# Row-halved projection matmuls in the last two attention units, joined value products and VectorE copies in the last one

## The chip, the cores and the metric

The kernel runs on one core of one Trainium2 chip. The metric is device time in microseconds (us) of one execution; three executions were timed and the median is given. The profile is of one further execution of the same program. Engines are named as in the profile: PE is TensorE's matmuls, PEld its weight loads, DVE is VectorE, ACT is ScalarE, POOL is GpSimd, SP is SyncE.

## The reference, cut to what matters

A transformer block in float32: pre-norm attention with 32 heads of 20 columns over 2048 tokens of width 640, then a pre-norm SwiGLU feed-forward of width 1728.

```
h  = x + attention(layernorm(x)) @ wo          # softmax over 2048 keys, 32 heads
h2 = h + (silu(n @ w_gate) * (n @ w_up)) @ w_down   # n = layernorm(h)
```

The change touches the stretch in which the last heads' attention runs while the first tokens' output projection (`@ wo`, added to x), their layernorm, and the transposition of the normed tokens for the feed-forward are already under way.

## The kernel before

**Stages.** The first stage (up to about 330 us) makes queries, keys and values. The second is attention. The third, from about 1471 us, finishes the projection and runs the feed-forward.

**Units and key tiles.** Attention runs over 32 units `u` (0 to 31): a unit is a group of four heads and a chunk `c` of 512 query tokens, `u = 4 * group + c`. Each unit has 16 key tiles `kt` of 128 keys. For every key tile PE makes four score products (`scores`, L1336: contraction over 62 rows, in one or the other half of the 128 rows, 512 columns, each into a `ps_one` bank of four), ACT takes the exponential of each (`probs`, L1342), and PE weighs the values with the probabilities of the key tile before (`weigh`, L1346: four products of 128 rows and 32 output columns each, which the trace shows as eight instructions). Finished probabilities wait in the list `todo`; `weigh_next` takes the oldest entry. The pool of `probs` has six tiles, two for each key tile.

**Row maxima.** Softmax needs the row maxima of a unit ahead of it. They come from further products (`max_one`, L229, 60 rows in one half, 512 columns) into a bank of `ps_max`, which DVE reduces (L235). `ps_max` has three banks in rotation. Three such products go into each key tile until all are done, which is in unit 30 after about ten key tiles; unit 31 has none.

**Order in a key tile.** PE's order is written out by hand: a string of `ORDER` for each key tile, of which s and S are score products in the lower and upper half of the rows, m and M maxima in the lower and upper half, and W is the weighing; with no maxima left it is `sSsSW`. After the weighing, at W, one entry of the list `extra` is issued.

**`extra`.** In units 30 and 31 it holds the output projection, norm and transposition of the chunks 0 and 1 (`projection(0, ...)` in unit 30, `projection(1, ...)` in unit 31): eight steps `first` in key tiles 0 to 7 (each a `project` of 128 tokens and one half of the 640 output columns), three steps of norm moments in key tiles 8 to 10, one empty step, and four `flip` steps in key tiles 12 to 15. A `project` issues 15 matmuls of 128 rows by 320 columns (L1070) into one `ps_max` bank; then DVE adds the sum to `h` (L1076), takes its moments (L1077), and after the second half of the columns combines them (L1079). A `flip` first issues the norm of the next token tile on DVE (`apply`, L1090), then five transposes (L1102) into two `ps_max` banks, and `split` copies each bank with ACT into a rounded high part and lets DVE subtract for the low part (both at the helper's lines L88 and L89).

In order on PE, in every key tile of units 30 and 31 that has a `project`: score and maximum products, W, 15 projection products. The next tile's score products follow. What stands behind the attention on PE is the projection of chunk 2 (`projection(2, ps_b)`), whose first product starts at 1470.88 us. The banks for it belong to a new pool, opened after the last weighing.

Of the kernel before, what the change touches and what calls it, by code (L numbers as in the profile page):

```python
# [9 lines left out]
F32 = mybir.dt.float32  # L10
# [4 lines left out]
ALU = mybir.AluOpType  # L15
AX = mybir.AxisListType

P = 128
# [5 lines left out]
ND = D // P  # L24
NT = S // P
CH = 512
NC = S // CH
# [7 lines left out]
ROW = P // 2  # L35
HALF = D // 2
# [11 lines left out]
def tile_block(ctx: ExitStack, tc: tile.TileContext, x, wqkv, wo, wg, wu, wd, out):  # L48
    nc = tc.nc
    x = x[0]  # L50
    out = out[0]
# [35 lines left out]
    def split(src, hi, lo, lo_engine=nc.vector):  # L87
        nc.scalar.activation(hi, src, AF.Copy)  # L88
        lo_engine.tensor_tensor(out=lo, in0=src, in1=hi.bitcast(F32), op=ALU.subtract)  # L89
# [38 lines left out]
    NU = NG * NC  # L128
# [906 lines left out]
        nc.gpsimd.tensor_copy(hi, raw)  # L1035
        nc.gpsimd.tensor_tensor(out=lo, in0=raw, in1=hi.bitcast(F32), op=ALU.subtract)

    def projection(c, ps_of):

        loaded, zs = {}, {}  # L1040
        mv = mvs[c] = moments_of[c // 2][:, c % 2]
        st = pe1.tile([P, TPC, 2, 6], F32, name=f"st{c}")
        rs = []

        def load(t):
            rows = slice((c * TPC + t) * P, (c * TPC + t + 1) * P)
            o = pc.tile([P, ND, P], F32, name="o_t", tag="o_t")
            nc.sync.dma_start(o, o_d[:, rows].rearrange("(k p) n -> p k n", p=P))
            loaded[t] = o

        def load_x(first=0, last=TPC):
            for t in range(first, last):
                rows = slice((c * TPC + t) * P, (c * TPC + t + 1) * P)
                nc.sync.dma_start(h_c[c][:, t, :], x[rows, :])

        def part(t):
            o = loaded[t]
            o_hi = pc.tile([P, ND, P], F32R, name="o_hi")
            o_lo = pc.tile([P, ND, P], F32R, name="o_lo")
            split(o, o_hi, o_lo, nc.gpsimd)  # L1060
            loaded[t] = (o_hi, o_lo)

        def project(t, half):
            o_hi, o_lo = loaded[t]
            hs = slice(half * HALF, (half + 1) * HALF)
            ps = ps_of()
            n = 0
            for a, w in ((o_hi, wo_hi), (o_hi, wo_lo), (o_lo, wo_hi)):
                for k in range(ND):
                    nc.tensor.matmul(  # L1070
                        ps[:, :HALF], a[:, k, :], w[:, k, hs],
                        start=(n == 0), stop=(n == 3 * ND - 1),
                    )
                    n += 1
            h = h_c[c][:, t, hs]
            nc.vector.tensor_tensor(out=h, in0=ps[:, :HALF], in1=h, op=ALU.add)  # L1076
            nc.vector.bn_stats(st[:, t, half, :], h)  # L1077
            if half == 1:
                nc.vector.bn_aggr(mv[:, t, :], st[:, t])  # L1079

        def moments(i):
            if i == 0:
                r, steps = rstd_steps(pc, mv[:, :, 1], TPC, "c")
                rs[:] = r, steps
            for f in rs[1][6 * i : 6 * i + 6]:
                f()

        def apply(t):
            z = zs[t] = pc.tile([P, D], F32, name="z2")
            nc.vector.tensor_scalar(  # L1090
                z, h_c[c][:, t, :], mv[:, t, 0:1], rs[0][:, t : t + 1],
                op0=ALU.subtract, op1=ALU.mult,
            )

        def flip(t):
            if t + 1 < TPC:
                apply(t + 1)
            z = zs.pop(t)
            for k0, k1 in ((0, 4), (4, 5)):
                ps = ps_of()  # L1100
                for k in range(k0, k1):
                    nc.tensor.transpose(  # L1102
                        ps[:, (k - k0) * P : (k - k0 + 1) * P], z[:, k * P : (k + 1) * P], ident
                    )
                if k1 < ND:
                    src = ps.rearrange("p (q k n) -> p q k n", q=2, n=P)
                    dst = both_of(z2_c[c])[:, :, t]
                    split(src, dst[:, :, 0], dst[:, :, 1], nc.vector)
                else:
                    dst = rest_of(z2_c[c])[:, t]  # L1110
                    split(ps[:, :P], dst[:, 0], dst[:, 1], nc.vector)

        def first(t, half):
            project(t, half)
            if half == 0 and t + 1 < TPC:
                part(t + 1)
            if half == 0 and t + 2 < TPC:
                load(t + 2)

        return (  # L1120
            [lambda: load(0), lambda: load(1), lambda: part(0)],
            [lambda t=t, half=half: first(t, half) for t in range(TPC) for half in range(2)],
            [lambda: moments(0), lambda: moments(1), lambda: apply(0)],
            [lambda t=t: flip(t) for t in range(TPC)],
            load_x,
        )
# [290 lines left out]
    for u in range(NU):  # L1417
        g, c = divmod(u, NC)
        if g == NG - 1 and c >= 2:
            _, first, ln, flips, _ = ahead  # L1420
            extra = [*first, *ln, lambda: None, *flips]
        for kt in range(NT):
            now[0] = u * NT + kt
            ready = [v for v, at in closing.items() if at == now[0]]
            probs = [pp.tile([P, 2, CH], F32, name="probs") for _ in range(2)]
            heads = [[0, 2], [1, 3]]
            order = ORDER[now[0] % len(ORDER)] if singles[0] or singles[1] else "sSsSW"
            for op in order:
                if op in "mM":
                    next_max(int(op == "M"))  # L1430
                elif op in "sS":
                    scores(u, kt, heads[op == "S"].pop(0), probs)
                else:
                    if todo:
                        weigh_next()
                    while ended:
                        max_all(ended.pop())
                    for v in ready:
                        max_finish(v)
                    if extra:  # L1440
                        extra.pop(0)()
                    if preparing and u and kt not in (3, 4) and quiet[0] != now[0]:
                        preparing.pop(0)()
                    if now[0] == (NU - NC) * NT + 8:
                        unit_ring, last_ring = weight_rings()
                        unit_ring.fill()
                        last_ring.fill()
            todo.append((u, kt, probs))
            if kt == 2 and u + 3 < NU:
                load_queries(u + 3)  # L1450
            if kt == 10 and u == 0:
                fill_ones(k_stk[1])
            if kt >= 8 and kt % 2 == 0 and c == 1 and g + 1 < NG:
                load_keys(g + 1, slice((kt - 8) // 2 * CH, (kt - 6) // 2 * CH))
            if kt >= 8 and kt % 2 == 0 and c == 2 and g + 1 < NG:
                load_values(g + 1, (kt - 8) // 2 * TPC, (kt - 6) // 2 * TPC)

            sooner = u >= NU - 2
            if kt == (3 if sooner else 4) and tail:
                reciprocals(u - 1, tail[0][2], nc.sync)  # L1460
                rb = spread(u - 1, nc.sync)
            if kt == (6 if sooner else 9) and tail:
                store_o(u - 1, tail[0][1], rb, nc.gpsimd, None)
            if kt == (7 if sooner else 11) and tail:
                store_o(u - 1, tail.pop()[1], rb, None, nc.sync)
            if g == NG - 1 and c >= 1:
                at = 8 if sooner else NT - 4
                if kt == at:
                    ahead = projection(
                        c - 1, ps_max if c < NC - 1 else (lambda: ps_b())  # L1470
                    )
                if kt in (at, at + 1, 12 if sooner else 14):
                    ahead[0][min(kt - at, 2)]()
                    if kt == at + 1 and c < NC - 1:
                        ahead[4]()
            k = 2 * (u - NU + 8)
            if kt in (12, 13) and 0 <= k + kt - 12 < ND:
                if k + kt == 12:
                    assert not preparing
                    wo_hi = pc.tile([P, ND, D], F32R, name="wo_hi", bufs=1)  # L1480
                    wo_lo = pc.tile([P, ND, D], F32R, name="wo_lo", bufs=1)
                load_wo(k + kt - 12)
            if kt in (2, 3) and 0 <= k + kt - 4 < ND:
                split_wo(k + kt - 4)
# [4 lines left out]
    u, o, r = tail.pop()  # L1489
# [6 lines left out]
    def ps_b():  # L1496
        return psum2.tile([P, CH], F32, name="ps_b", tag="ps_b", bufs=4)
# [551 lines left out]
```

## Time and profile before

| | us |
|---|---|
| median of three executions | 2038.6 (2038.28 to 2039.58) |
| the profiled execution, its own time | 2035.66 |
| span of the profiled execution, first to last instruction | 2033.9 |
| mean granted TensorE clock | 0.997 |
| PE busy | 2008.8 (99%) |
| DVE busy | 1612.6 (79%) |
| ACT busy | 1462.4 (72%) |
| POOL busy | 785.7 (39%) |

Busy PE counts pipelined matmuls from modelled start to end, so that PE looks busy in a drain too; how long a stretch takes is read from the starts of instructions. In the timeline a row is a run of like instructions of one engine: start, time to the end of the last, engine, line, operation, output and inputs, shapes, count, and in brackets the idle time before it with what ended it. A table by stretches gives for each engine the busy time and the count of instructions.

### The profile page before, as it was taken

The numbers are of one execution on the slowest core, as the hardware profiler recorded it, in microseconds if no ns is written. First come the engines' busy times: TensorE is split into PE (matmuls) and PEld (weight loads), VectorE is DVE, ScalarE is ACT, GpSimd is POOL, SyncE is SP. The second block draws the span as 40 slices with busy tenths as digits, with TensorE's granted clock in tenths as the row PEclk, the third lists the DMA queues.
The fourth block names the chain that finished last, engine by engine and source line by source line (L and its number), as shares of the span: only waits on it lengthen the run. The fifth ranks groups of instructions, "written<-read, shape, count | busy, mean of one in ns | idle before, by whom it ended". The sixth has DMA issues, their size and how long they took to land. (4 is left out here: it accounts for less than half of the span.)

```text
span 2033.9 us, 39129 instructions
## 1 busy us (share of the span) xinstructions
PE 2008.8 (99%) x13716; PEld 1238.9 (61%) x13716; DVE 1612.6 (79%) x3241; ACT 1462.4 (72%) x2952; POOL 785.7 (39%) x1079
## 2 busy tenths in 40 slices
PE   7999999999999999999999999999999999999999
PEld 6899996333333333333333333345598888888888
DVE  6678788888888888888888888885377666676677
ACT  3788988999999999999999999987633222211221
POOL 5554450334434334344430011011145454744555
PEclk9999999999999999999999999999999999999999
DMA  7776663343443534444433123211158654974642
GB/s 227 243 222 186 203 185 100 113 128 99 150 124 113 163 123 138 129 141 146 141 126 109 30 65 80 83 62 49 41 193 292 222 193 156 346 272 159 202 151 95
DMA packets 205124, 305.03 MB, mean 150 GB/s; under 512 B 47664, under 2 KB 82480, under 8 KB 203904
## 3 DMA queue, kind: packets, MB, share of 16 engines
q1 hardware_dynamic: 204832, 302.53, 45.9%
q8 instruction: 109, 1.79, 0.4%
q14 instruction: 87, 0.71, 0.1%
q10 hardware_dynamic: 96, 0.00, 0.0%
HBM read 205.78 MB, written 95.68 MB: 148 GB/s over the span
## 5 line engine op out<-in xcount | busy, mean ns | idle before, releaser
L1342 ACT ACTIVATE probs<-ps_one 128x512 f32<-128x512 f32 x2048 | 1056.9, 615 | 62.0 <-PE ps_one L1336 24.2
L235 DVE TENSOR_REDUCE mx<-ps_max 128x1 f32<-128x512 f32 x1472 | 925.4, 684 | 116.2 <-PE ps_max L229 64.1
L1336 PE MATMUL ps_one<-q_stk,k_stk 62*128 62x512 f32 x2048 | 583.5, 431 | 1.2 <-DVE mx L199 1.2
L1346 PE MATMUL acc<-probs,v_stk 128*32 128x512 f32 x4096 | 546.7, 605 | 0.0
L229 PE MATMUL ps_max<-k_stk,q_stk 60*128 60x512 f32 x1472 | 488.7, 440 | 0.1
L1336 PEld LDWEIGHTS ps_one<-q_stk,k_stk 62*128 62x128 f32 x2048 | 290.5, 185 | 284.7 <-ACT probs L1342 269.7
L229 PEld LDWEIGHTS ps_max<-k_stk,q_stk 60*128 60x128 f32 x1472 | 245.2, 185 | 165.4 <-DVE mx L235 126.9
L1729 DVE TENSOR_TENSOR tmp<-ps_a,tmp 128x512 f32<-128x512 f32 x208 | 141.3, 690 | 122.1 <-PE ps_a L1514 96.4
L1346 PEld LDWEIGHTS acc<-probs,v_stk 128*32 128x32 f32 x4096 | 80.6, 108 | 181.7 <-issue 169.5
L1608 PE MATMUL ps_b<-halves,yp 128*128 128x320 f32 x1032 | 179.0, 308 | 1.5 <-POOL yp L89 1.3
L1608 PEld LDWEIGHTS ps_b<-halves,yp 128*128 128x128 f32 x1032 | 165.2, 188 | 17.5 <-POOL yp L89 1.5
L1514 PE MATMUL ps_a<-t,units 128*128 128x512 f32 x624 | 162.5, 396 | 0.0
L246 POOL CAST both<-neg 128x16 fp32r<-128x16 f32 x32 | 6.6, 207 | 361.6 <-PE ps_one L1336 153.7
L1514 PE MATMUL ps_a<-z,units 128*128 128x512 f32 x516 | 133.9, 394 | 0.0
L89 POOL TENSOR_TENSOR yp<-y,yp 128x256 fp32r<-128x256 f32 x96 | 60.2, 627 | 189.8 <-ACT yp L88 189.8
L1514 PEld LDWEIGHTS ps_a<-t,units 128*128 128x128 f32 x624 | 112.6, 188 | 18.5
L1613 DVE TENSOR_TENSOR h<-ps_b,h 128x320 f32<-128x320 f32 x248 | 110.0, 482 | 6.9 <-PE ps_b L1608 5.4
L216 DVE CUSTOM_DVE_ANT_0 q_stk<-ps_single,q_stk 128x512 f32<-128x512 f32 x143 | 95.7, 689 | 22.4 <-ACT q_stk L222 15.0
L1514 PEld LDWEIGHTS ps_a<-z,units 128*128 128x128 f32 x516 | 93.1, 187 | 16.0
L556 PE MATMUL ps_one<-z_hi,w_hi 64*128 64x512 f32 x380 | 99.1, 402 | 1.8 <-ACT z_hi L88 1.7
L88 ACT ACTIVATE yp<-tmp 128x512 fp32r<-128x512 f32 x40 | 25.3, 632 | 103.2 <-POOL tmp L1601 103.2
L1381 POOL TENSOR_TENSOR o<-o,rb 128x512 f32<-128x512 f32 x31 | 39.9, 1286 | 152.9 <-ACT probs L1342 55.8
(221 smaller groups left out, 3017.9 us busy)
## 6 DMA issues: line engine op xcount, KB each, us to landing
units<-w_d SPq DMA_DIRECT2D x186, 256.0 KB
w_d<-stage SPq DMA_DIRECT2D x106, 256.0 KB
halves<-j_d SPq DMA_DIRECT2D x70, 320.0 KB
k_stk<-qk_d SPq DMA_DIRECT2D x112, 160.0 KB
j_d<-stage SPq DMA_DIRECT2D x42, 320.0 KB
q_stk<-qk_d SPq DMA_DIRECT2D x64, 160.0 KB
k_stk<-qk_d SPq DMA_DIRECT2D x112, 80.0 KB
rb<-r_d SPq DMA_DIRECT2D x32, 256.0 KB
```

The lines of the kernel that those rows point to most:

```text
L89: lo_engine.tensor_tensor(out=lo, in0=src, in1=hi.bitcast(F32), op=ALU.subtract)
L216: nc.vector.tensor_tensor_reduce(out=place, in0=pss[1], in1=place, scale=1.0, scalar=LEAST, op0=ALU.add, op1=ALU.max, accum_out=mx[:, b, p ...
L229: nc.tensor.matmul(ps, queries[u][rows, pair, t * P : (t + 1) * P], keys[u // NC][rows, pair, kc * CH : (kc + 1) * CH], start=True, stop=True,
L235: nc.vector.tensor_reduce(mxs[u][:, b, pair, t, kc : kc + 1], ps, axis=AX.X, op=ALU.max)
L556: product = nc.tensor.matmul(job["ps"][:, :out], lhs, rhs, start=(half == 0 and i == 0), stop=(half == 1 and i == job["n"] - 1),)
L1336: nc.tensor.matmul(ps, keys[u // NC][rows, p, kt * P : (kt + 1) * P], queries[u][rows, p, :], start=True, stop=True,)
L1342: nc.scalar.activation(probs[p][:, b, :], ps, AF.Exp, scale=scale)
L1346: nc.tensor.matmul(acc[32 * j : 32 * j + 32, :], values[u // NC][:, kt, j * VW : j * VW + 32], probs[j // 2][:, j % 2, :], start=(kt == 0) ...
L1514: nc.tensor.matmul(ps.rearrange("p (t n) -> p t n", t=TPC), w[k][:, i], z[k][:, :, j], start=(first and m == 0), stop=(last and m == len(n ...
L1608: nc.tensor.matmul(ps, a, b, start=(n == 0), stop=(n == len(pairs) - 1))
L1613: nc.vector.tensor_tensor(out=h, in0=ps, in1=h, op=ALU.add)
L1729: add = lambda out, ps, x: nc.vector.tensor_tensor(out=out, in0=ps, in1=x, op=ALU.add)
```

## The change

Three edits.

1. `projection` gets an argument `halved`. With it `project` makes each of its 15 products as two, one over the rows 0 to 63 and one over the rows 64 to 127, each row half into a bank of its own, the two halves in turn; DVE then adds both banks to `h`, one after the other. It is set for chunks 0 and 1, so in units 30 and 31; chunks 2 and 3 keep whole products.
2. In unit 31 the weighing is done in even key tiles only, two entries of `todo` there (one in key tile 0, which finds one entry), none in odd key tiles but the last, which takes one.
3. In `flip` of chunk 1 (unit 31) the copy of the high part is DVE's instead of ACT's; chunk 0 keeps ACT.

```
-    def projection(c, ps_of):
+    def projection(c, ps_of, halved=False):
...
             hs = slice(half * HALF, (half + 1) * HALF)
-            ps = ps_of()
+            rows = [slice(b * ROW, (b + 1) * ROW) for b in range(2)] if halved else [slice(0, P)]
+            pss = [ps_of() for _ in rows]
             n = 0
             for a, w in ((o_hi, wo_hi), (o_hi, wo_lo), (o_lo, wo_hi)):
                 for k in range(ND):
-                    nc.tensor.matmul(
-                        ps[:, :HALF], a[:, k, :], w[:, k, hs],
-                        start=(n == 0), stop=(n == 3 * ND - 1),
-                    )
+                    for r, ps in zip(rows, pss):
+                        nc.tensor.matmul(
+                            ps[:, :HALF], a[r, k, :], w[r, k, hs],
+                            start=(n == 0), stop=(n == 3 * ND - 1),
+                        )
                     n += 1
             h = h_c[c][:, t, hs]
-            nc.vector.tensor_tensor(out=h, in0=ps[:, :HALF], in1=h, op=ALU.add)
+            for ps in pss:
+                nc.vector.tensor_tensor(out=h, in0=ps[:, :HALF], in1=h, op=ALU.add)
             nc.vector.bn_stats(st[:, t, half, :], h)
...
                     dst = both_of(z2_c[c])[:, :, t]
-                    split(src, dst[:, :, 0], dst[:, :, 1], nc.vector)
+                    hi, lo = dst[:, :, 0], dst[:, :, 1]
                 else:
                     dst = rest_of(z2_c[c])[:, t]
-                    split(ps[:, :P], dst[:, 0], dst[:, 1], nc.vector)
+                    src, hi, lo = ps[:, :P], dst[:, 0], dst[:, 1]
+                if c == 0:
+                    split(src, hi, lo, nc.vector)
+                else:
+                    nc.vector.tensor_copy(hi, src)
+                    nc.vector.tensor_tensor(out=lo, in0=src, in1=hi.bitcast(F32), op=ALU.subtract)
...
                 else:
-                    if todo:
-                        weigh_next()
+                    both = u == NU - 1 and kt < NT - 1
+                    for _ in range(2 * (1 - kt % 2) if both else 1):
+                        if todo:
+                            weigh_next()
...
                     ahead = projection(
-                        c - 1, ps_max if c < NC - 1 else (lambda: ps_b())
+                        c - 1, *((ps_max, True) if c < NC - 1 else (lambda: ps_b(),))
                     )
```

## The prediction, made before the changed kernel ran

> **What bounds the kernel now.** I read the table by stretches first, cut at the key tiles that matter: the eight tiles of unit 30 with a projection, the rest of unit 30, the eight tiles of unit 31 with a projection, and the rest up to the first product behind the attention. The columns are time, then PE, PEld, DVE, ACT and POOL busy with counts, clock and DMA.
>
> ```profile
> 1361.70:1398.96 37.26, 37.26 (x244) 23.80 (x240) 22.31 (x45) 19.20 (x37) 5.98 (x4) 1.00 0.26 83
> 1398.96:1418.61 19.65, 19.54 (x126) 7.83 (x123) 12.61 (x31) 18.91 (x42) 2.53 (x3) 1.00 0.01 4
> 1418.61:1449.64 31.03, 31.03 (x210) 20.86 (x206) 7.75 (x18) 17.97 (x35) 5.96 (x4) 1.00 0.20 57
> 1449.64:1470.88 21.24, 20.50 (x126) 7.40 (x125) 10.05 (x26) 19.96 (x42) 1.55 (x1) 1.00 0.01 1
> ```
>
> PE is full and ACT half idle wherever a projection runs (stretches 1 and 3); ACT is the bound in the other two (18.91 of 19.65, 19.96 of 21.24). So one change meets two regimes. Behind 1470.88, the same view over the rest of the program:
>
> ```profile
> sum 564.00, PE 555.45 PEld 487.95 DVE 395.89 ACT 131.97 POOL 297.61; mean PE 50.50 PEld 44.36 DVE 35.99 ACT 12.00 POOL 27.05
> ```
>
> PE has 8.6 us of 564 free and nothing else is full: a shift of the attention's end goes through to the end one for one. The sum below is therefore the shift of that end.
>
> Next the timeline of unit 30, PE alone and DVE alone, for the steps of one tile; the waits of PE's weight loads; and mean durations from the page.
>
> ```profile
> 1363.27 0.90 PE L1070 MATMUL ps_max<-wo_hi,o_lo 128*128 128x320 f32 x5
> ...
> 1365.42 1.06 PE L1346 MATMUL acc<-probs,v_stk 128*32 128x512 f32 x8
> 1366.42 0.85 PE L1070 MATMUL ps_max<-wo_hi,o_hi 128*128 128x320 f32 x4
> ```
> ```profile
> 1364.20 0.49 DVE L1076 TENSOR_TENSOR h<-ps_max,h 128x320 f32<-128x320 f32 x1 [2.45 <-PE ps_max L1070]
> 1364.73 0.49 DVE L1077 BATCH_NORM_STATS2 st<-h 128x6 f32<-128x320 f32 x1
> 1365.14 1.87 DVE L235 TENSOR_REDUCE mx<-ps_max 128x1 f32<-128x512 f32 x3
> ...
> 1369.97 0.21 DVE L1079 BATCH_NORM_AGGREGATE mvs<-st 128x2 f32<-128x12 f32 x1
> 1370.10 1.83 DVE L235 TENSOR_REDUCE mx<-ps_max 128x1 f32<-128x512 f32 x3
> ```
> ```profile
> PEld ps_max L229 <- DVE h L1076: 2.1, 6, 0.4
> ```
> ```profile
> L235 DVE TENSOR_REDUCE mx<-ps_max 128x1 f32<-128x512 f32 x1472 | 925.4, 684 | 116.2 <-PE ps_max L229 64.1 <-PE ps_one L1336 48.3
> L1336 PE MATMUL ps_one<-q_stk,k_stk 62*128 62x512 f32 x2048 | 583.5, 431 | 1.2 <-DVE mx L199 1.2
> L1346 PE MATMUL acc<-probs,v_stk 128*32 128x512 f32 x4096 | 546.7, 605 | 0.0
> ```
>
> Already now a maximum product waits for the bank that DVE's add has to empty (six times, up to 0.4 us): with three `ps_max` banks, DVE's queue is nearly on PE's path.
>
> **Edit 1, the halves themselves.** Whether two row halves stream side by side is shown by the first stage:
>
> ```profile
> 302.32 0.31 PE L556 MATMUL ps_one<-w_lo,z_hi 64*128 64x320 f32 x1
> 302.41 0.66 PE L556 MATMUL ps_one<-w_hi,z_lo 64*128 64x320 f32 x6
> ```
>
> One such half product lasts 0.31, six of both halves 0.66, so they start (0.66 - 0.31) / 5 = 0.07 apart, 0.14 for a pair. A whole product steps by (0.90 - 0.31) / 4 = 0.147 (row at 1363.27). Thirty halves cost what fifteen whole ones do, 2.2 us. What can be gained is at the end:
>
> ```profile
> 1424.29 0.90 PE L1070 MATMUL ps_max<-wo_hi,o_lo 128*128 128x320 f32 x5
> 1425.12 0.76 PE L1336 MATMUL ps_one<-q_stk,k_stk 62*128 62x512 f32 x4
> 1425.81 1.06 PE L1346 MATMUL acc<-probs,v_stk 128*32 128x512 f32 x8
> 1426.80 0.42 PE L1070 MATMUL ps_max<-wo_hi,o_hi 128*128 128x320 f32 x1
> ```
>
> The last whole product starts at 1424.29 + 0.59 = 1424.88, the scores 0.24 later instead of one step of 0.147; and the second pair of scores starts 0.76 - 0.43 = 0.33 after the first, against about 0.23 where halves run on (estimate: 0.147 x 512/320), 0.10 more. Halves are of the scores' kind, so both go: 0.09 + 0.10, taken as 0.195 for a projection, 1.6 us for eight.
>
> **Edit 1 in unit 30, the banks.** Let P be the start of the last projection product, 1363.27 + 0.59 = 1363.86. DVE's add starts P + 0.34, the moments 0.53 later, the first reduction 0.41 after that, the others by (1.87 - 0.68) / 2 = 0.60. The next projection starts at 1366.42 = P + 2.56. Its bank is that of the first maximum, whose reduction ends at 1365.14 + 0.68 = P + 1.96. No wait.
>
> Now the projection takes two of three banks, the three maxima take the third and then those two, and the next projection wants the banks of the first and the second maximum. DVE's queue has a second add, which needs the first one's result; I price that as moments after add, 0.53. So: first add P + 0.34, second 0.87, moments 1.40, reductions 1.81 and 2.41, the second ending at 3.09. With 0.05 for PE to see it (an estimate: DVE sees PE's end, 1363.86 + 0.31, within 0.03) the second half starts at P + 3.14, not 2.56. PE works in order, so the first half's next product, the rest of this projection and the next scores are queued behind it. From there 2.16 us to the new P as now (1361.70, where the first stretch is cut, to 1363.86). The cycle is 5.30; after a second column half the combining (0.53 after the moments if priced like them, the reductions 0.13 after it, instead of 0.41) adds 0.25: 5.55. Eight projection tiles take 37.26 now, 4.66 each. Over seven cycles: 4 x 5.30 + 3 x 5.55 - 7 x 4.66 = **+5.2 us**. The 0.195 is inside this, since PE comes earlier and waits longer; the eighth tile's is used up by the third maximum, which waits for the second add. Bounds: -1.6 if no bank is late, +6.5 if the third maximum delays the weighing by another 0.2 in each cycle. I take 5.2: every term is a row, and the cycle closes on itself.
>
> A sentence of the Trainium skill speaks to this. In "TensorEngine Tiling (Array Packing)", section "Gotcha 1: PSUM Pressure", it says that row tiles write to different banks and cannot use one bank at the same time. Without that rule one bank and one add would do and unit 30 would gain 1.6; with it, it loses 5.2; no run here shows two halves in one bank at once.
>
> **Edit 1 in unit 31.** No maxima, DVE idle (7.75 of 31.03): the gain stands, **-1.6 us**.
>
> **Edit 2, tiles 0 to 8.** A weighing takes 1.00 to the next kind of product, two passes of (1.06 - 0.61) = 0.45 in it. A second one directly behind costs 0.91 and saves a change into weighing (last scores to weighing 0.36 instead of 0.23, from 1425.12 + 0.33 to 1425.81: 0.13) and the slow first steps after it (0.1 each for projection and scores): 0.4 a pair. But in an odd tile two projections are only 0.47 of scores apart: the second one's second bank is free at 0.34 + 0.49 + 0.05 = 0.88 after the last product, PE is there at 0.147 + 0.47 = 0.62. That gives back 0.26. Four pairs: **-0.6 us** (between 0 and -1.6).
>
> **Edits 2 and 3, tiles 8 to 15.** Here ACT is the bound:
>
> ```profile
> 1453.73 1.04 PE L1336 MATMUL ps_one<-q_stk,k_stk 62*128 62x512 f32 x4
> ...
> 1457.80 1.04 PE L1336 MATMUL ps_one<-q_stk,k_stk 62*128 62x512 f32 x4
> 1458.78 1.06 PE L1346 MATMUL acc<-probs,v_stk 128*32 128x512 f32 x8
> 1459.77 0.76 PE L1102 MATMUL ps_max<-ident,z 128*128 128x128 f32 x5
> 1460.47 0.73 PE L1336 MATMUL ps_one<-q_stk,k_stk 62*128 62x512 f32 x4
> ```
> ```profile
> 1450.19 10.21 ACT L1342 ACTIVATE probs<-ps_one 128x512 f32<-128x512 f32 x20 [2.02 <-PE ps_one L1336]
> ...
> 1463.65 0.82 ACT L88 ACTIVATE z<-ps_max 128x512 fp32r<-128x512 f32 x2
> 1464.28 1.16 ACT L1342 ACTIVATE probs<-ps_one 128x512 f32<-128x512 f32 x2
> ```
>
> Twenty exponentials in 10.21 without a break: 2.04 a tile, two tiles 4.07 (1453.73 to 1457.80). Four `ps_one` banks hold one tile, so when the last score of a tile goes out ACT has 2.04 us of work. PE returns with scores 0.36 + 1.00 later, and ACT starts on the first 0.55 after (1449.64, the cut at tile 8's first score, to 1450.19): 1.91, just in time. With two weighings 0.36 + 1.91 + 0.55 = 2.82: ACT runs dry 0.8 us a pair. Tiles 8 to 12 hold two pairs, the first with ACT idle at its start: +0.8 and +0.4. From tile 12, PE's chain of first score, paced last score (0.55), 0.36, weighings 1.91, transposes 0.70 (1459.77 to 1460.47), scores 13 at 3.5, whose flip waits 0.35 for DVE to free a bank, scores 14 with the last at 6.3 behind ACT, 2.27, 0.70, scores 15, one weighing, flip, weighing gives 13.9 to the product behind the attention, against 13.1 now (1457.80 to 1470.88): +0.9. That holds edit 3: the copies leave ACT (0.63 a flip, 1463.65 to 1464.28, 2.5 for four), but ACT no longer bounds these tiles. On DVE they cost what a subtraction does, 0.69 and 0.28, since copy and add cost the same at 320 columns:
>
> ```profile
> L1629 DVE COPY own<-ps_b 128x320 f32<-128x320 f32 x32 | 14.2, 481 | 0.4 <-PE ps_b L1608 0.4
> L1076 DVE TENSOR_TENSOR h<-ps_max,h 128x320 f32<-128x320 f32 x16 | 7.9, 492 | 37.6 <-PE ps_max L1070 37.6
> ...
> L89 DVE TENSOR_TENSOR z<-ps_max,z 128x512 fp32r<-128x512 f32 x8 | 5.5, 691 | 16.7 <-ACT z L88 16.7
> ```
>
> DVE's last pair ends under the last weighing. Together **+2.1 us** (between -2.5, ACT's relief whole, and +3.2, with DVE freeing banks later).
>
> **Sum.** 5.2 - 1.6 - 0.6 + 2.1 = +5.1 us. On the profiled execution's 2035.66 that is 2040.8; the median of the runs is 2.9 above that execution, so I forecast 2038.6 + 5.1 = **2043.7 us**. A measurement of this kernel can tell about 0.2%, 4.1 us, from no change.
>
> **Rivals.** (a) *Only mode changes count; faster.* DVE is quick enough: were the second reduction over 0.8 us earlier (3.14 - 2.36), no bank would be late. Then -1.6 in unit 30, -1.6 and -1.6 in unit 31, -2.5 from ACT: -7.3, 2031.3; with half of ACT's and the pairs' part, 2033.5. The 0.24 in place of 0.147 speaks for it, the rows of DVE against. The skill's "TensorEngine Tiling (Array Packing)", "Key Properties", is of this kind: a change of tiling mode drains the array, a change of tile doesn't. Chance 0.15. (b) *The bank wait is real, the joined weighing costs nothing and ACT's relief is whole*: 5.2 - 2.2 - 2.5 = +0.5, 2039.1; or DVE starts the second add at half the price and unit 30 loses 3. For it: ACT is full at 1450 to 1471. Chance 0.25. (c) *Halves do not run side by side* in these units: 16 x 2.2 = +35, 2074. Against it the first stage's 0.14 a pair; 0.02.
>
> **How the numbers follow.** My case, both losses about as sized (2042.7 to 2046.5), has 0.58. Faster by over 0.2%: 0.15; within: 0.25; slower: 0.60. The range from 2034.5 to 2047.0 leaves out most of (a), all of (c) and little above.
>
> **What would show it.** Right: in unit 30 eight tiles near 5.3 to 5.5 us, the products L1070 waiting for the reductions L235, a second add 0.53 behind the first; in unit 31 odd tiles of about 2.9 and pairs of 7.9; gaps near 0.8 in ACT behind joined weighings. Wrong: unit 30 at 4.5 a tile or below, or ACT gapless to 1470.

## The result, and the profile after

The changed kernel took 2044.86 us (median of 21 executions, 2039.68 to 2048.73), the one before 2039.43 us beside it: a ratio of 1.0028 (95% interval 1.0020 to 1.0036), or 4 to 7 us slower. Ratios here and below leave out one execution of 2187.55 us, of the kernel with the copies alone, that stood 7% above its others. The forecast was +5.1 us with a chance of 0.60 for slower. The profiled execution of after took 2041.89 us, span 2040.1, clock 0.997 as before.

The table by stretches of after, cut at the same events as before (time, then PE, PEld, DVE, ACT and POOL busy with counts, clock and DMA):

```profile
1362.82:1405.75 42.93, 40.38 (x366) 24.86 (x362) 26.24 (x53) 19.83 (x37) 5.99 (x4) 1.00 0.23 73
1405.75:1425.41 19.66, 19.55 (x126) 7.82 (x123) 12.59 (x31) 18.92 (x42) 2.53 (x3) 1.00 0.01 2
1425.41:1453.89 28.48, 28.48 (x319) 21.64 (x317) 11.19 (x25) 18.07 (x35) 5.97 (x4) 1.00 0.18 48
1453.89:1477.09 23.20, 21.32 (x138) 7.82 (x134) 13.05 (x35) 17.41 (x34) 1.55 (x1) 1.00 0.06 19
```

Against before, stretch by stretch: +5.67, +0.01, -2.55, +1.96, together +5.1. Behind the last cut both kernels need 563.0 us (2040.1 - 1477.09 and 2033.9 - 1470.88), so the shift of the attention's end does go through to the end. The span differs by 6.2; the other 1.1 lies ahead of the first cut (1362.82 against 1361.70), where the code is the same. One correction to the cuts: the first one ends at the first score of key tile 9, not 8, because the scores of tile 8 follow the eighth projection directly. It is the same event in all kernels, and the lengths of the cycles are taken between projection starts.

Unit 30, PE and then DVE of after, one cycle:

```profile
1364.39 0.90 PE L1072 MATMUL ps_max<-wo_hi,o_lo 64*128 64x320 f32 x10
...
1365.87 0.50 PE L229 MATMUL ps_max<-k_stk,q_stk 60*128 60x512 f32 x1 [0.35 <-DVE h L1079]
...
1366.46 0.50 PE L229 MATMUL ps_max<-k_stk,q_stk 60*128 60x512 f32 x1
...
1367.13 1.06 PE L1354 MATMUL acc<-probs,v_stk 128*32 128x512 f32 x8
1368.12 1.05 PE L1072 MATMUL ps_max<-wo_hi,o_hi 64*128 64x320 f32 x10
```
```profile
1365.32 1.09 DVE L1079 TENSOR_TENSOR h<-ps_max,h 128x320 f32<-128x320 f32 x2 [2.45 <-PE ps_max L1072]
1366.44 0.49 DVE L1080 BATCH_NORM_STATS2 st<-h 128x6 f32<-128x320 f32 x1
1366.85 1.87 DVE L235 TENSOR_REDUCE mx<-ps_max 128x1 f32<-128x512 f32 x3
```

With P the start of the last projection product, 1364.39 + 0.59 = 1364.98, the next projection starts at 1368.12 = P + 3.14; before it was P + 2.56. The row of the two adds gives 1.09 - 0.49 = 0.60 from one to the next. The second maximum starts 0.06 after the first add's end (1365.32 + 0.49), the third 0.05 after the second's (1365.32 + 1.09): these two maxima wait, and scores, weighing and projection are queued behind them on PE. The weighing then takes its ordinary 0.99 to the projection.

The waits of PE's weight loads in this stretch, and two rows of those loads from a cycle in which DVE also combines the moments:

```profile
PEld ps_max L229 <- DVE h L1079: 7.9, 16, 0.7
PEld ps_max L1072 <- DVE mx L235: 7.3, 10, 0.8
```
```profile
1384.06 0.18 PEld L1072 LDWEIGHTS ps_max<-wo_hi,o_hi 64*128 64x128 f32 x1 [0.84 <-DVE mx L235]
1384.54 0.73 PEld L1072 LDWEIGHTS ps_max<-wo_hi,o_hi 64*128 64x128 f32 x9 [0.29 <-DVE mx L235]
```

The wait of a maximum for an add was 2.1 us in six times and is 7.9 in sixteen. Of the projection's waits for the reductions, the 0.84 in brackets lies under the weighing and was there before too; what is new is the second row: here the first half's product went out at 1384.06, and the second half's had to wait until 1384.54.

Unit 31, PE of after, through one pair of key tiles:

```profile
1433.17 1.00 PE L1072 MATMUL ps_max<-wo_hi,o_hi 64*128 64x320 f32 x10
...
1435.47 0.63 PE L1344 MATMUL ps_one<-q_stk,k_stk 62*128 62x512 f32 x4
1435.94 1.27 PE L1072 MATMUL ps_max<-wo_hi,o_hi 64*128 64x320 f32 x10
...
1438.38 0.76 PE L1344 MATMUL ps_one<-q_stk,k_stk 62*128 62x512 f32 x4
1439.07 1.92 PE L1354 MATMUL acc<-probs,v_stk 128*32 128x512 f32 x16
1440.92 1.00 PE L1072 MATMUL ps_max<-wo_hi,o_hi 64*128 64x320 f32 x10
```

A pair takes 1440.92 - 1433.17 = 7.75. Its second projection, only 0.47 of scores behind the first, needs 1.27 for its first ten halves instead of 1.00 (the bank of its second half is not yet added), and the scores behind that one take 0.76 instead of 0.63.

The last tiles, ACT of after, and DVE's copies by their forms:

```profile
1454.33 2.06 ACT L1350 ACTIVATE probs<-ps_one 128x512 f32<-128x512 f32 x4 [0.84 <-PE ps_one L1344]
1456.98 4.03 ACT L1350 ACTIVATE probs<-ps_one 128x512 f32<-128x512 f32 x8 [0.59 <-PE ps_one L1344]
1461.91 4.03 ACT L1350 ACTIVATE probs<-ps_one 128x512 f32<-128x512 f32 x8 [0.91 <-PE ps_one L1344]
...
1467.55 4.03 ACT L1350 ACTIVATE probs<-ps_one 128x512 f32<-128x512 f32 x8 [0.99 <-PE ps_one L1344]
```
```profile
L1118 DVE CAST z<-ps_max 128x512 fp32r<-128x512 f32 x4 | 2.8, 690 | 8.9 <-PE ps_max L1105 8.9
...
L1118 DVE CAST z<-ps_max 128x128 fp32r<-128x128 f32 x4 | 1.1, 280 | 0.0
```

ACT, which did twenty exponentials without a break before, now stops after every pair of key tiles.

### The profile page after: what moved, and what is told of

Its sections match the earlier page's. It is cut to its first block, busy times and chain, and to the rows that moved or that the text cites. A ratio compares the mean times of both kernels' runs of the same rounds, so it can differ in the third digit from the quotient of the medians.

```text
span 2040.1 us, 39643 instructions
## 1 busy us (share of the span) xinstructions
PE 2009.9 (99%) x13956; PEld 1239.7 (61%) x13956; DVE 1620.7 (79%) x3265; ACT 1460.4 (72%) x2944; POOL 786.1 (39%) x1079
```

## The experiments

All edits are against the changed kernel. Stretches 1 to 4 are the four of the table; before had 37.26, 19.65, 31.03 and 21.24.

**The halves in unit 30 alone, and in unit 31 alone.**

```
# h30: the flag is c == 1; h31: the flag is c == 2
-                        c - 1, *((ps_max, True) if c < NC - 1 else ...
+                        c - 1, *((ps_max, c == 1) if c < NC - 1 else ...
# both: weighings one by one, ACT's copies
-                    both = u == NU - 1 and kt < NT - 1
+                    both = False
-                if c == 0:
+                if c <= 1:
```

> Row halves in unit 30 alone. Stretches are read between the same events in every kernel: 1 from the first projection product of unit 30 to the first score of its tile 8 (37.3 us before, 42.9 after), 2 from there to the first projection product of unit 31 (19.7, 19.7), 3 to the first score of tile 8 of unit 31 (31.0, 28.5), 4 to the first product behind the attention (21.2, 23.2). Theory (three banks and a longer DVE queue): stretch 1 is 42.9 as in the changed kernel, the others as before, total +5.5 us. Rival (the loss of the changed kernel is in the joined weighings and the copies, halves only save mode changes): stretch 1 is 35.7 to 37.3, total 0 to -1.6.

> Row halves in unit 31 alone. Theory: where no maxima share the banks the halves save one change of mode in each projection, 0.195 us: stretch 3 from 31.0 to 29.5, the others as before, total -1.6 us. Rival (a second add and two banks cost anywhere): stretch 3 at 31.0 or longer.

Measured: h30 1.0030 (1.0020 to 1.0039), h31 0.9981 (0.9965 to 0.9996). Stretch 1 of h30, and stretch 3 of h31 with its PE rows for one key tile:

```profile
1363.79:1406.73 42.94, 40.38 (x365) 24.90 (x362) 26.26 (x53) 19.83 (x37) 5.97 (x4) 1.00 0.24 73
```
```profile
1420.14:1449.44 29.30, 29.30 (x328) 20.89 (x326) 11.19 (x25) 17.95 (x35) 5.95 (x4) 1.00 0.16 46
```
```profile
1427.86 1.00 PE L1072 MATMUL ps_max<-wo_hi,o_hi 64*128 64x320 f32 x10
...
1430.16 0.63 PE L1344 MATMUL ps_one<-q_stk,k_stk 62*128 62x512 f32 x4
1430.72 1.06 PE L1354 MATMUL acc<-probs,v_stk 128*32 128x512 f32 x8
1431.71 0.56 PE L1072 MATMUL ps_max<-wo_hi,o_hi 64*128 64x320 f32 x4
```

The same edit loses 5.7 us beside the maxima (42.94 against 37.26) and gains 1.7 without them (29.30 against 31.03). The gain is where the forecast put it: scores directly behind halves take 0.63 instead of 0.76, and the weighing follows 0.56 after the first score instead of 0.69. The Trainium skill's "TensorEngine Tiling (Array Packing)", "Key Properties", says that a change of tiling mode drains the array; these rows agree, with about 0.2 us for the change that is saved in each key tile (1.73 / 8).

**The joined weighings alone, and the copies alone.**

```
# both: whole products
-                        c - 1, *((ps_max, True) if c < NC - 1 else ...
+                        c - 1, *((ps_max, False) if c < NC - 1 else ...
# joined: ACT's copies
+                if c <= 1:
# copies: weighings one by one
+                    both = False
```

> Joined weighings in unit 31 alone. Theory: with whole projections stretch 3 shrinks by 0.6 to 1.6 us (29.4 to 30.4; no second bank to wait for), and stretch 4 grows by 3 (to about 24.3) because ACT runs dry 0.8 us behind each joined weighing and still has the copies to make; total +1.5 to +2.6. Rival (a change of mode less is a gain everywhere): stretch 4 at 21.2 or less, total -1.5 to -2.5.

> The copies of the turned tokens by DVE alone. Theory: ACT is the bound of stretch 4 while weighings are single, so that stretch shrinks by about 1.0 us (to 20.2), less than the 2.5 us of copies that ACT loses, since DVE's chain of copy, subtraction and norm then frees the banks later; the others as before, total -1.0. Rival one (ACT's relief goes through whole): stretch 4 at 18.7. Rival two (DVE becomes the bound): 21.2 or more.

Measured: joined 1.0014 (1.0005 to 1.0024), copies 0.9993 (0.9983 to 1.0003). Stretches 3 and 4 of joined, and stretch 4 of copies:

```profile
1421.78:1451.18 29.40, 29.40 (x200) 20.97 (x197) 7.75 (x18) 17.95 (x35) 5.99 (x4) 1.00 0.19 56
1451.18:1478.51 27.33, 25.42 (x133) 8.41 (x133) 10.06 (x26) 20.06 (x42) 1.54 (x1) 0.88 0.02 6
```
```profile
1457.23:1477.27 20.04, 19.29 (x125) 7.23 (x125) 12.57 (x34) 17.50 (x34) 1.57 (x1) 1.00 0.00 1
```

The copies on DVE gain 1.2 us in stretch 4 of the profile (20.04 against 21.24). The joined weighings gain 1.6 in stretch 3, and lose 6.1 in stretch 4, far more than they do in after. The clock column tells why: 0.88. PE of joined at that place:

```profile
1451.85 1.92 PE L1354 MATMUL acc<-probs,v_stk 128*32 128x512 f32 x16
1453.70 0.74 PE L1344 MATMUL ps_one<-q_stk,k_stk 62*128 62x512 f32 x4
1454.89 1.97 PE L1344 MATMUL ps_one<-q_stk,k_stk 62*128 62x512 f32 x4 [0.45 <-ACT probs L1350]
1456.78 3.60 PE L1354 MATMUL acc<-probs,v_stk 128*32 128x512 f32 x16
...
1463.39 3.46 PE L1354 MATMUL acc<-probs,v_stk 128*32 128x512 f32 x16
```

The same sixteen products took 1.92 us once and 3.60 and 3.46 later: 3.2 us of the 6.1. Of the 1.6 gained, about 0.9 is a weighing that stands in stretch 4 instead (below).

**Joined, with PE kept busy.** Six products that nothing reads are added behind the scores of the odd key tiles 9, 11 and 13 of unit 31, where the weighing stood; the joined kernel's other edits stay.

```
+                    if u == NU - 1 and kt >= 8 and kt % 2 and kt < NT - 1:
+                        for n in range(6):
+                            rows = slice(n % 2 * ROW, n % 2 * ROW + NPART)
+                            nc.tensor.matmul(
+                                ps_max(), keys[g][rows, 0, :P], queries[u][rows, 0, :],
+                                start=True, stop=True,
+                            )
```

> Joined weighings alone, with six extra products of 60 rows by 512 columns (nobody reads them) behind the scores of tiles 9, 11 and 13, where PE has nothing to do. In the profile of joined the granted clock fell to 0.5 twice for 3.4 us in stretch 4 (27.3 us where 24.3 was expected), and two joined weighings there took 3.5 to 3.6 us instead of 1.92. Theory (PE too idle between joined weighings lets the clock fall): with PE filled the clock stays at 1.0 and stretch 4 is 24.3 to 24.8 us. Rival (the joined weighing itself brings the clock down): it falls again and stretch 4 is 27 or more.

Measured: 1.0025 (1.0015 to 1.0036). Stretch 4:

```profile
1453.27:1477.28 24.01, 23.22 (x151) 9.78 (x150) 10.07 (x26) 20.06 (x42) 1.56 (x1) 1.00 0.01 2
```

In the profile the fall is gone, clock 1.00, and with it 3.3 us (24.01 against 27.33). So at full clock the joined weighings alone cost 24.01 - 21.24 = 2.8 in stretch 4, and with the 1.6 gained in stretch 3 about 1.1 in all. The timed runs do not confirm a cure: this kernel is no faster than joined, and the intervals overlap. They also put it 3 to 7 us behind before, more than these 1.1; what makes up the rest is open. A profile is of one execution, so how often the clock falls in joined is open.

**The stop in unit 30 taken apart.** One kernel has the halves in unit 30 with only the first bank added (h30 as above, and):

```
-            for ps in pss:
+            for ps in pss[:1]:
```

> Row halves in unit 30 alone, and of the two adds of each projection there only the first (the second half of the sum is left out of the output). Stretch 1 from the first projection product of unit 30 to the first score of its tile 9 (37.3 us before, 42.9 in the changed kernel). Theory (bank rotation and DVE's queue together): the reductions come 0.53 earlier, the second bank is free at P + 2.61 instead of 3.14, the cycle is about 4.77 (5.02 after a second column half), so stretch 1 is 38.5 to 39 us: the second add has 4 of the 5.6 us. Rival one (the banks alone: two of three taken): 42 to 43. Rival two (DVE alone): 35.7 to 36.

Two others give the maxima a fourth bank at the cost of one for the scores, one with h30's halves and one with none:

```
-        return psum.tile([P, CH], F32, name="ps_one", tag="ps_one", bufs=4)
+        return psum.tile([P, CH], F32, name="ps_one", tag="ps_one", bufs=3)
-        return psum.tile([P, CH], F32, name="ps_max", tag="ps_max", bufs=3)
+        return psum.tile([P, CH], F32, name="ps_max", tag="ps_max", bufs=4)
```

> Row halves in unit 30 alone with four banks for maxima and projections, taken from the scores' four, which leaves them three. Read against the same split of banks with whole projections (before_four_banks), stretch 1 only. Theory: the next projection then needs the second half's own old bank and that of the first maximum, free at P + 2.54 instead of 3.14, so the cycle is about 4.7 (4.95) and stretch 1 is longer than in before_four_banks by 0.5 to 1.5 us, not 5.6. Rival (DVE's longer queue by itself costs the time): longer by 5 or more.

> The kernel before with four banks for maxima and projections and three for scores: the control for h30_four_banks. Theory: stretch 1 is bound by PE and stays at 37 to 38.5 us; the rest of the attention, bound by ACT, gets longer by an amount that I can't price. Rival: stretch 1 grows as well, since a score then waits for an exponential of its own tile.

Measured, one execution each: 2038.47 us for one add, 2294.44 with four banks and halves, 2296.98 with four banks and none. Stretch 1 of the three, in this order:

```profile
1363.48:1401.65 38.17, 38.02 (x365) 24.89 (x362) 22.32 (x45) 19.19 (x37) 5.96 (x4) 1.00 0.26 81
```
```profile
1600.68:1639.91 39.23, 38.34 (x364) 24.99 (x360) 25.74 (x52) 18.97 (x36) 5.99 (x4) 1.00 0.26 80
```
```profile
1603.43:1643.55 40.12, 38.30 (x245) 24.25 (x242) 22.59 (x45) 18.99 (x36) 6.00 (x4) 1.00 0.25 77
```

Without the second add 4.8 of the 5.7 us are gone (38.17, where 38.5 to 39 was expected), though PE still issues every half and takes two banks. In that kernel nothing reads the second bank, so two things go at once, the add's time in DVE's queue and its hold on the bank; the run does not part them. By the profile the maxima's wait for an add falls from 7.9 us in sixteen times to 1.9 in eight, while the projection's wait for the reductions is 7.3 in ten times in both. With a fourth bank both adds stay, and the halves cost nothing against their control (39.23 against 40.12) and even gain 0.9; I had expected a small loss to stay. So DVE's longer queue alone is not the cost, it is that queue with only three banks. The control is not a clean one, though: it took 40.12 where 37 to 38.5 was expected, so its rival held. With three banks of their own the scores wait for the exponentials, more without halves than with them, and what the halves add can hide in that wait. These are the weight loads' waits in that stretch, with halves and without:

```profile
PEld ps_one L1344 <- ACT probs L1350: 2.0, 5, 0.7
```
```profile
PEld ps_one L1344 <- ACT probs L1350: 6.2, 9, 0.8
```

As a way out it is none: with three score banks the whole kernel is over 250 us slower.

**Everything but unit 30's halves, and two versions built from the parts that gain.**

```
# all three: halves in unit 31 only
+                        c - 1, *((ps_max, c == 2) if c < NC - 1 else ...
# h31_copies
+                    both = False
# h31_join6_copies
+                    both = u == NU - 1 and kt <= 6
```

> The changed kernel with whole projections in unit 30. Theory: stretch 1 is back at 37.3, stretches 3 and 4 are 28.5 and 23.2 as in the changed kernel; the attention ends 0.6 us earlier than before, total -0.6 (no change that can be measured). Rival (edits 2 and 3 lose by themselves): total +1 or more, as it would be if the clock fell in stretch 4 (+3).

> Row halves in unit 31 and copies by DVE, single weighings, whole projections in unit 30: the two edits that gained alone. Theory: the gains add, stretch 3 is 29.3, stretch 4 is 20.0, total -2.9 us. Rival (DVE, with a second add in each tile before, gets behind): stretch 4 at 21.

> As h31_copies, with joined weighings in tiles 2, 4 and 6 of unit 31, where PE is the bound, and single ones from tile 7 on. Theory: the wait for the second bank in odd tiles takes back what the mode changes save, stretch 3 is 29.2 to 29.6 and stretch 4 is 20.0: nothing over h31_copies. Rival (the joined weighing is a gain wherever PE is the bound, 0.4 us a pair): stretch 3 is 28.1, total -4.1.

Measured: 1.0005 (0.9996 to 1.0014), 0.9986 (0.9977 to 0.9994; medians 2034.58 against 2038.26) and 0.9988 (0.9976 to 1.0000). Stretches 1, 3 and 4 of the first, 3 and 4 of the second, 3 of the third:

```profile
1361.93:1399.22 37.29, 37.29 (x244) 23.82 (x240) 22.33 (x45) 19.19 (x37) 5.97 (x4) 1.00 0.27 83
1418.88:1447.39 28.51, 28.51 (x320) 21.68 (x317) 11.20 (x25) 18.07 (x35) 5.96 (x4) 1.00 0.17 50
1447.39:1470.59 23.20, 21.31 (x137) 7.82 (x134) 13.06 (x35) 17.42 (x34) 1.56 (x1) 1.00 0.06 16
```
```profile
1421.95:1451.27 29.32, 29.32 (x329) 20.93 (x326) 11.20 (x25) 17.95 (x35) 5.99 (x4) 1.00 0.17 48
1451.27:1471.18 19.91, 19.16 (x128) 7.12 (x125) 13.06 (x35) 17.50 (x34) 1.57 (x1) 1.00 0.07 21
```
```profile
1418.19:1447.62 29.43, 29.43 (x328) 21.76 (x326) 11.20 (x25) 18.07 (x35) 5.97 (x4) 1.00 0.21 59
```

With whole projections in unit 30 and the rest of the change in place, stretch 1 is back at 37.29 and stretch 4 stays at 23.20, both as expected: the loss of the changed kernel goes with unit 30's halves. Unit 31's halves with DVE's copies gain 1.7 + 1.3 = 3.0 us in the profile and 2.9 by the ratio of the runs, less than the 0.2% that the prediction names, though the interval excludes no change. h31, without the copies and timed at another time, has 0.9981, and the two intervals overlap: the runs do not show that the copies add to the halves. Joining the weighings of tiles 2 to 6 adds nothing to it: 29.43 against 29.32. The 28.51 of all_but_h30 is no gain of the join either. Joined up to tile 8, stretch 3 holds six weighings instead of seven, and the seventh (0.9 us) stands in stretch 4, in tile 8's double one.

## Why the prediction was right

The total came out closer than its parts. In the profile the attention's end moved by 5.1 us, as forecast, but unit 30 cost 0.5 more than forecast and unit 31 0.5 less (-0.6 where the terms give -0.1). That the two cancel is luck.

**Unit 30, forecast +5.2, measured +5.7.** Length and cause held. First add P + 0.34, as forecast; second add 0.60 behind the first instead of 0.53; moments P + 1.46 for 1.40; first reduction P + 1.87 for 1.81. The first cycle, between the first two projection starts, is 1368.12 - 1362.82 = 5.30, as forecast, and the seven together are 37.62 (to 1400.44) where I had 37.85; before they were 32.55, so +5.1. From first add to first add the plain cycles take 5.21 to 5.31 and the three with combining 5.43, 5.63 and 5.43, for 5.30 and 5.55. The other 0.6 lies in the eighth tile, for which I had counted nothing: its maxima wait for the adds like those of the seven others (sixteen waits, two in each tile). One step was misnamed: I let the cycle close on the second half's bank, which waits for the second reduction, and gave the maxima's wait for the adds a part only in the eighth tile. In the cycle shown the maxima's wait is what PE feels; it puts the projection at P + 3.14, and the reduction, which ends at 1366.85 + 1.27 = 1368.12, is just in time for the second half. In three of the four plain cycles the second half starts 0.05 to 0.06 behind the first, in one of them 0.30; where DVE also combines it waits 0.26 to 0.50 (0.48 at 1384.06). Both chains are DVE's, both go through the second add, and in those three cycles they end within 0.1 us of each other, which is why the number came out though the wait was misnamed. h30_one_add shows the second add as the cause of 4.8; how much the second half's wait would have cost without the maxima's is not shown. The Trainium skill's "TensorEngine Tiling (Array Packing)", under "PSUM Bottleneck", warns that tiling speeds up TensorE but not the emptying of its banks. In stretch 1 TensorE's own time stayed the same (0.90 for ten halves or five whole products) and the emptying got longer by an add; the trace agrees that the emptying then sets the pace, at 5.7 us. Whether two halves could share one bank wasn't tried.

**Unit 31's halves, forecast -1.6, measured -1.7.** Right in size and place.

**The join in tiles 0 to 8, forecast -0.6.** Stretch 3 shows -0.8 from it, but that is a weighing moved behind the cut, which I had not counted. The pair itself gains nothing: 7.75 in after against 2 x 3.85 in h31 (1427.86 to 1431.71). I had 0.4 saved and 0.26 given back by the late bank. What is given back is 0.27, as forecast (1.27 against 1.00): 0.14 of it on the way to the scores (1435.94 to 1438.38 is 2.44, against 2.30 in h31), and 0.13 in the scores (0.76 instead of 0.63), since the late second half leaves the two rows of halves staggered. The mis-sized term is the saving. It is 0.22: 0.09 where projection follows scores directly (0.47, the weighing stood at 0.56) and 0.13 in the double weighing (1.85 against 2 x 0.99). joined, with whole products and no second bank to wait for, saves as little: 7.98 a pair (1429.75 to 1437.73) against 8.18 before (1426.80 to 1434.98).

**Tiles 8 to 15, forecast +2.1, measured +2.0.** The sum held, its split did not; both numbers hold the weighing that was moved. From tile 8's first score (1453.89) to tile 12's, and on to the product behind the attention (1477.09):

```profile
1462.57 1.97 PE L1344 MATMUL ps_one<-q_stk,k_stk 62*128 62x512 f32 x4 [0.45 <-ACT probs L1350]
1464.46 1.92 PE L1354 MATMUL acc<-probs,v_stk 128*32 128x512 f32 x16
```

Tiles 8 to 12 took 8.68 (before 8.16: +0.5, forecast +1.2), the rest 14.52 (before 13.08: +1.4, forecast +0.9). I let tile 12's last score go out 0.55 after its first, as before. It is paced by ACT for longer: the weighing stands 1.89 behind the first score instead of 0.55 + 0.36 = 0.91. ACT's lag is not lost in tiles 8 to 12 but carried into tile 12. The gaps of ACT are 0.59 to 0.99 where about 0.8 was forecast, and DVE's copies cost 0.690 and 0.280 us, as forecast. Alone they are worth 1.2 us (20.04 against 21.24); beside the joined weighings, where ACT runs dry anyway, about 0.8 (23.20 in after against joined_filled's 24.01, if the eighteen extra products cost nothing there, which was not tested).

**The rivals.** *Only mode changes count* is what unit 31 does and unit 30 doesn't. *The joined weighing costs nothing and ACT's relief is whole* fell: ACT's relief is 1.2, not 2.5, and the join loses 2.8 in stretch 4; nor did the second add start at half the price (0.60). *Halves not side by side* is out: stretch 3 of h31 is shorter, not 17 us longer.

## What to carry to other kernels

Here a product split into row halves cost TensorE nothing and saved a change of mode, but it took a second bank and a second, dependent add. It paid where the emptying engine was idle (1.7 us). Beside a chain of that engine's work that already ended just before TensorE wanted the bank, it cost about the extra add's start-to-start time, 0.6 us, in every turn, though DVE was busy for only 22.31 of 37.26 us there. So write out the other engine's queue for one whole turn and close the cycle, and close it over every bank that turn uses, since two waits can end together. When work is moved past the end of the stretch that you measure, compare over the next stretch too: here 0.9 us of apparent gain was a weighing counted elsewhere.

## What was not expected of the hardware

The granted clock fell to a half in joined's profile, in the middle of the attention, in two stretches of 3.41 us with 1.00 between them. The table over the run-up to the first fall and over both falls:

```profile
1453.39:1456.80 3.41, 2.96 (x15) 1.06 (x11) 2.28 (x9) 2.95 (x7) 0.00 (x0) 1.00 0.00 0
1456.80:1460.21 3.41, 3.41 (x17) 0.58 (x16) 0.00 (x0) 1.46 (x3) 0.00 (x0) 0.50 0.03 5
...
1463.63:1467.04 3.41, 3.41 (x17) 0.69 (x10) 0.00 (x0) 1.24 (x3) 0.00 (x0) 0.50 0.00 0
```

Ahead of the fall PE had nothing but eight score products in 3.08 us (1453.70 to 1456.78), half of them paced by ACT, and no gap longer than 0.45. The Trainium skill's "TensorE: Matmul & The Clock Gate", "Part 1: The HAM clock gate", tells of half rate after an idle window of about 3.4 us; length and depth agree with these rows, but there was no idle time of that length here, so a thin stretch seems to be enough. That is not shown to the end: after has the same thin stretch (scores at 1456.45 and 1457.63) at clock 1.00, and joined_filled, without one, has 1.00 too. Where the stretch falls in time may decide. In joined the clock's last change before was at 337.23, and from there to the fall at 1456.80 it is 328 steps of 3.413 us; the thin stretch fills one such step nearly whole (1453.39 to 1456.80), and so does the next one ahead of the second fall. In after and all_but_h30 the last change before was at 335.88 and 335.94; if the steps run on from there, a step ends inside each of their thin stretches, in after near 1458.9. The three executions fit that reading, and they are too few to show it.
